# Two short expert calls of an attention and mixture-of-experts kernel: one of them is moved out of a branch, both now stand behind the fifth and the sixth pair of blocks

## The chip, the cores and the metric

The kernel runs on one core of one Trainium2 chip. The metric is the time of one execution in microseconds (us), as the device measures it. The program computes first an attention layer and then a routed mixture of experts, in one launch.

## The reference

The attention has 4 batches, 8 heads, 768 positions and 64 columns for each head; each position sees a window of its neighbours and 24 block summaries. Its output is cut into rows of 512 columns, 3072 rows in all, and each row goes to one of eight experts:

```
e = fresh_e if (s == 0 or local_gate[b, s] < 0.5) else prev_e
h = np.maximum(x[b, s] @ w1[e], 0.0)      # 512 -> 1024
out[b, s] = p[e] * (h @ w2[e])            # 1024 -> 512
```

So which rows belong to which expert is known only while the program runs.

## The kernel before

The rows of an expert are gathered into blocks of 128 rows. The experts' part of the program works on blocks, each of them a "slot" with an expert and a list of rows; a program part of the routing works out the slots while the attention and the first blocks run, and writes them into `words` in SBUF.

**Pairs.** `pair` runs two blocks of one expert at once: 96 matmuls of the first layer (lines 1131 to 1133; tiles `bs<-xT`), then 48 of the second layer for each block (lines 1104 to 1106; `ba<-hT`), with the transposes of the next pair's rows (L1087; `bt<-ident,xg`) between them. Each product is made of three matmuls, since weights and rows are split into a high and a low part. Eight pairs are written out in straight-line code, without a condition on TensorE: the static part. Behind them stands the dynamic part: at each step the program reads a word and takes either a pair or `single` (one block alone, `If two > 0` and its `Else`, L1457), until no slots are left. In the run that is shown the first step of the dynamic part takes the `single`, then come two pairs, a second `single` and a last pair.

**Weights.** While a pair runs, the weights of the next expert are split from the stage buffers `stg` into high and low parts, by ScalarE (L1062), VectorE (L1065) and GpSimd (L1070), and the stage is then filled again by SyncE's queue (L1058), each under a condition on the expert being a new one. In the run that is shown the stage is requested in the seventh and the eighth pair and in the dynamic part.

**The 32-row calls.** Up to two experts have a remainder of under 32 rows. Such a remainder doesn't get a block: `few` computes it with its own weights. `few_in` requests the weights (`few_w`, two tiles of 2 MB, four requests of 1 MB), `few_gather` fetches the rows (GpSimd, L1197), `few_tx` transposes them (L1204) and `few` makes both layers (L1219, L1223, L1230) under a condition (L1431). In the program a call has 32 matmuls for each layer, and the trace shows each as two. There is one pair of weight tiles, so the weights of the second call can be requested only when the first call has read them. In the run that is shown both calls are needed.

**Order around the change.** Before, the first call's weights and rows are requested behind the fifth pair, and the call stands behind the sixth. The second call's first weight tile is requested behind the first call, its second tile behind the seventh pair, and the call itself stands in the dynamic part, at the head of its first step: once in the branch of the pair and once in that of the `single`, since only one of them runs.

Of the kernel before, what the change touches and what calls it, by code (L numbers as in the profile page):

```python
# [16 lines left out]
ENG = mybir.EngineType  # L17
# [14 lines left out]
KT, FT = DM // P, DF // P  # L32
G9 = E + 1
SLOTS = 42
PAIRS = 8
FEW = 32
FEWS = 2
ALL = SLOTS + FEWS
CALLS = 12
EARLY = 6  # L40
FEW_TX = 5
FIRST = 10
OOB = 4096
WARM = 44
# [25 lines left out]
class Kernel:  # L70
# [1167 lines left out]
    def run(self):  # L1238
# [35 lines left out]
        def freed():  # L1274
            st["free"] += 1
            have_rows(0, st["rows"])
# [6 lines left out]
        def stage_e1():  # L1283
            for w in range(2):
                refill(w, st["e1"])
# [41 lines left out]
        def reg(i, engines, hi):  # L1327
            return nc.values_load(self.words[0:1, i:i + 1], engines=engines, min_val=0, max_val=hi)

        def refill(w, nxt):  # L1330
            for h in range(2):
                self.fetch(st["stage"][w][:, 2048 * h:2048 * h + 2048], w, 2048 * h, 2048 * h + 2048, nxt)

        def split(w, chunks):
            for q in chunks:
                eng = nc.vector if SPLIT_BY[w][q] == "V" else nc.gpsimd
                self.split(w, q * CH, q * CH + CH, st["stage"][w][:, q * CH:q * CH + CH], eng)

        def calls(n):

            r = {}

            def start(s):
                while "words" not in st:
                    self.small(1, True)
                if s not in r:
                    r[s] = reg(s, (ENG.SP, ENG.Activation, ENG.DVE, ENG.Pool), 1), reg(SLOTS + s, (ENG.SP,), E - 1)
                return r[s]

            def weights(w, s, chunks):  # L1350
                if s == EARLY - 2:
                    split(w, chunks)
                    if chunks[-1] == NCH - 1:
                        st["spent"].append(w)
                        refills()
                if not EARLY <= s < SLOTS:
                    return
                new, nxt = start(s)
                with tc.If(new > 0):  # L1359
                    split(w, chunks)  # L1360
                    if chunks[-1] == NCH - 1:
                        refill(w, nxt)

            def mid(half):
                if n < SLOTS:
                    while st["next"] <= n + half:
                        self.small(1, True)
                    if half and n >= 2 * PAIRS:
                        with tc.If(reg(n + 1, (ENG.PE, ENG.Activation, ENG.DVE), 1) > 0):
                            self.tx(n + half, half)  # L1370
                    else:
                        self.tx(n + half, half)
                    freed()

            return mid, lambda *chunks: weights(0, n, chunks), lambda *chunks: weights(1, n, chunks)
# [11 lines left out]
        with ExitStack() as ctx:  # L1387
            self.fw = ctx.enter_context(tc.tile_pool(name="f_wk", bufs=1))
            sp = ctx.enter_context(tc.tile_pool(name="stage", bufs=1))
            places = ctx.enter_context(ExitStack())  # L1390
            self.gw = places.enter_context(tc.tile_pool(name="g_wk", bufs=1, side="right"))
            st["spent"] = []
            st["stage"] = [sp.tile([P, KT * DF], F32, name=f"stg{w}") for w in range(2)]

            if "e1" in st:
                stage_e1()

            def refills():
                if "words" in st:
                    while st["spent"]:  # L1400
                        refill(st["spent"].pop(0), st["words"])

            def have_words():
                st["words"] = reg(SLOTS + EARLY - 2, (ENG.SP,), E - 1)
                refills()

            self.have_words = have_words
            rest = chain(first, *(self.pair(i, *calls(2 * i + 2)) for i in range(1, FEW_TX)))
            while self.steps:
                next(rest, None)  # L1410
                self.flow(C_T)
            for _ in rest:
                pass
            assert "words" in st and self.have_p == SLOTS
            places.close()
            fp = ctx.enter_context(tc.tile_pool(name="few", bufs=1, side="right"))
            self.few_w = [fp.tile([P, KT * DF], F32, name=f"few_w{w}") for w in range(2)]
            self.few_x = fp.tile([FEW, DM], F32, name="few_x")
            self.few_xT = fp.tile([P, KT, FEW], F32, name="few_xT")

            def few_reg(j, engines, hi=1):
                return nc.values_load(self.few_words[0:1, j:j + 1], engines=engines, min_val=0, max_val=hi)

            def few_in(j, chunks):
                used, e = few_reg(j, (ENG.SP,)), few_reg(FEWS + j, (ENG.SP,), E - 1)
                with tc.If(used > 0):
                    for q in chunks:
                        self.few_in(q, e)

            def few(j):  # L1430
                with tc.If(used[j] > 0):  # L1431
                    self.few(j)

            self.few_gather(0)
            few_in(0, range(4))
            for i in range(FEW_TX, PAIRS):
                for k, _ in enumerate(self.pair(i, *calls(2 * i + 2))):
                    if k == 2 * FT:
                        if i == FEW_TX:
                            self.few_tx()  # L1440
                            self.few_gather(1)
                        if i == PAIRS - 1:
                            self.few_tx()
                if i == FEW_TX:
                    used = [few_reg(j, (ENG.PE, ENG.Activation, ENG.DVE, ENG.Pool)) for j in range(FEWS)]
                    nb = reg(2 * SLOTS, mybir.ALL_ENGINES, SLOTS)
                    few(0)
                    few_in(1, range(2))
                if i == FEW_TX + 1:
                    few_in(1, range(2, 4))  # L1450
            with ExitStack() as c:  # L1451
                for i in range(2 * PAIRS, SLOTS, 2):
                    if i >= 2 * CALLS:
                        c.enter_context(tc.If(nb > i - EARLY))
                    two = reg(i + 1, mybir.ALL_ENGINES, 1)
                    kept = dict(st)
                    with tc.If(two > 0) as full:  # L1457
                        if i == 2 * PAIRS:
                            few(1)
                        for _ in self.pair(i // 2, *calls(i + 2)):  # L1460
                            pass
                    st.update(kept)
                    with full.Else():
                        if i == 2 * PAIRS:
                            few(1)
                        self.single(i, *calls(i + 2))


# [81 lines left out]
```

## Time and profile before

| | |
|---|---|
| time, median of 3 runs | 463.37 us (462.78 to 464.55) |
| the profiled execution's own time | 466.23 us |
| its span in the trace | 464.5 us |
| TensorE busy | 424.6 us, 91% of the span |
| ScalarE, VectorE, GpSimd busy | 202.4, 250.5 and 216.8 us |

The span is what the trace shows from the first instruction to the last; the execution's own time has 1.73 us more. The profiled execution is 2.86 us longer than the median of the three timed runs. A share of busy time is a mean over stages that differ; what a change in one stage is worth is read from that stage.

### The profile page before, as it was taken

Reading aid. Unit: us, or ns where it says so; the run is one execution under the profiler, and the core shown is the slowest. Engines: PE = TensorE matmul, PEld = TensorE weight load, DVE = VectorE, ACT = ScalarE, POOL = GpSimd, SP = SyncE. Lnnn points to the kernel's source line nnn. Section 1 sums busy time; section 2 is a strip of 40 time slices with the busy share of each in tenths; the row PEclk is TensorE's granted clock in tenths of the full one; section 3 lists DMA queues with packets and bytes.
Section 4 is the critical chain, followed back from the end, with each engine's and each line's share of the span. In section 5 each row is a group of like instructions: output and inputs, shape, how many; then the busy total and the mean of one; then the engine's idle time right before and its main releaser. Section 6 shows DMA issues by size and latency. Waiting matters only on the chain. (4 is left out here: it accounts for less than half of the span.)

```text
span 464.5 us, 12258 instructions
## 1 busy us (share of the span) xinstructions
PE 424.6 (91%) x4512; PEld 369.0 (79%) x4512; DVE 250.5 (54%) x610; ACT 202.4 (44%) x454; POOL 216.8 (47%) x305
## 2 busy tenths in 40 slices
PE   7799989889699999999999999999959999999980
PEld 6588868767489798898989898989847898977960
DVE  5776797888855798993222222155441722356410
ACT  4788787887635125421212121154431821358200
POOL 2687676687404423932030312149491652097620
PEclk9989999999889999999999999999997999999996
DMA  8999989989230660472920202508974472058930
GB/s 307 368 384 389 387 253 404 394 318 324 89 141 2 236 262 25 157 285 82 359 73 24 68 30 76 206 25 280 347 265 179 148 283 94 0 205 294 344 124 26
DMA packets 24009, 95.87 MB, mean 206 GB/s; under 512 B 2895, under 2 KB 3537, under 8 KB 19313
## 3 DMA queue, kind: packets, MB, share of 16 engines
q1 hardware_dynamic: 19328, 80.30, 46.4%
q0 software_dynamic: 4448, 14.29, 9.2%
q8 instruction: 43, 0.70, 0.6%
q14 instruction: 46, 0.37, 0.2%
q10 hardware_dynamic: 144, 0.20, 0.1%
HBM read 82.20 MB, written 12.71 MB: 204 GB/s over the span
## 5 line engine op out<-in xcount | busy, mean ns | idle before, releaser
L1131 PE MATMUL bs<-xT,h 128*128 128x256 f32 x352 | 101.2, 287 | 0.0
L1133 PE MATMUL bs<-xT,l 128*128 128x256 f32 x352 | 99.8, 284 | 0.7 <-DVE l L1065 0.5
L1132 PE MATMUL bs<-xT,h 128*128 128x256 f32 x352 | 99.7, 283 | 0.2 <-DVE xT L1082 0.2
L1076 POOL DMA_INDIRECT xg<-x_dram,gidx x30 | 35.1, 1170 | 102.2 <-POOLq L1359 43.2
L1137 ACT ACTIVATE hT<-bs 128x512 fp32r<-128x512 f32 x44 | 26.3, 597 | 110.1 <-PE bs L1133 107.6
L1104 PE MATMUL ba<-h,hT 128*128 128x512 f32 x176 | 71.5, 406 | 0.4
L1106 PE MATMUL ba<-h,hT 128*128 128x512 f32 x176 | 68.8, 391 | 0.0
L1105 PE MATMUL ba<-l,hT 128*128 128x512 f32 x176 | 68.7, 391 | 0.0
L1133 PEld LDWEIGHTS bs<-xT,l 128*128 128x128 f32 x352 | 67.4, 191 | 1.3 <-DVE l L1065 1.3
L1131 PEld LDWEIGHTS bs<-xT,h 128*128 128x128 f32 x352 | 67.4, 191 | 1.1 <-issue 0.6
L1132 PEld LDWEIGHTS bs<-xT,h 128*128 128x128 f32 x352 | 67.4, 192 | 0.9 <-DVE xT L1082 0.7
L1139 DVE SCALAR_TENSOR_TENSOR hT<-bs,hT 128x512 fp32r<-128x512 f32 x44 | 30.3, 690 | 68.9 <-ACT hT L1137 57.8
L1070 POOL TENSOR_TENSOR l<-stg,h 128x256 fp32r<-128x256 f32 x72 | 63.1, 907 | 7.6 <-ACT h L1062 6.9
L291 ACT ACTIVATE pr<-bs,nm 128x120 f32<-128x120 f32 x192 | 51.7, 370 | 12.0 <-DVE nm L287 11.5
L1062 ACT CAST h<-stg 128x1024 fp32r<-128x1024 f32 x48 | 48.8, 1051 | 9.2 <-PE ba L1106 8.1
L1117 POOL DMA_INDIRECT out_dram<-yo,sidx x24 | 27.0, 1124 | 46.1 <-DVE yo L1116 17.2
L1065 DVE TENSOR_TENSOR l<-stg,h 128x1024 fp32r<-128x1024 f32 x30 | 40.7, 1367 | 13.5 <-ACT h L1062 10.3
L1104 PEld LDWEIGHTS ba<-h,hT 128*128 128x128 f32 x176 | 33.1, 188 | 7.5 <-ACT h L1062 0.6
L1106 PEld LDWEIGHTS ba<-h,hT 128*128 128x128 f32 x176 | 33.0, 188 | 7.3
L1105 PEld LDWEIGHTS ba<-l,hT 128*128 128x128 f32 x176 | 33.2, 189 | 5.5
L252 POOL COPY vw<-vs 24x384 f32<-24x384 f32 x64 | 32.3, 546 | 7.7 <-ACT vs L247 6.2
L287 DVE TENSOR_REDUCE nm<-bs 128x6 f32<-128x720 f32 x32 | 28.8, 901 | 9.2 <-ACT vs L247 4.0
(278 smaller groups left out, 681.8 us busy)
## 6 DMA issues: line engine op xcount, KB each, us to landing
stg<-in_w SPq DMA_DIRECT2D x28, 1024.0 KB, 6.7
vw<-in_vW SPq DMA_DIRECT2D x16, 780.0 KB, 7.4
few_w<-in_w SPq DMA_DIRECT2D x8, 1024.0 KB, 8.9
kp<-in_kT SPq DMA_DIRECT2D x16, 384.0 KB, 6.5
q<-in_qT SPq DMA_DIRECT2D x16, 384.0 KB, 7.0
vt<-in_vT SPq DMA_DIRECT2D x16, 384.0 KB, 7.5
x_dram<-xs SPq DMA_DIRECT2D x8, 768.0 KB, 5.1
wst<-in_w SPq DMA_DIRECT2D x8, 512.0 KB, 6.9
```

The costliest lines, as they stand in the source:

```text
L252: nc.gpsimd.tensor_copy(out=vw[n % 3][WL:W, t:t + NW // 4, :, 0:D], in_=vs.to_broadcast([NB, NW // 4, 2, D]))
L291: nc.scalar.activation(out=pr[:, h, u, :], in_=sp[:, h, u, :], func=AF.Exp, bias=nm[:, h, u:u + 1], scale=1.0)
L1062: self.nc.scalar.copy(out=hi, in_=src)
L1065: eng.tensor_tensor(out=lo, in0=src, in1=hi.bitcast(F32), op=ALU.subtract)
L1070: eng.tensor_tensor(out=lo[:, p], in0=src[:, p], in1=hi[:, p].bitcast(F32), op=ALU.subtract)
L1076: self.nc.gpsimd.indirect_dma_start(out=t, out_offset=None, in_=rows, in_offset=bass.IndirectOffsetOnAxis(ap=self.gidx[:, i:i + 1], axis=0))
L1104: nc.tensor.matmul(out=ps, lhsT=ah, rhs=wh, start=first, stop=False)
L1105: nc.tensor.matmul(out=ps, lhsT=ah, rhs=wl, start=False, stop=False)
L1106: nc.tensor.matmul(out=ps, lhsT=al, rhs=wh, start=False, stop=last)
L1131: nc.tensor.matmul(out=ps[:, j], lhsT=wh, rhs=xh, start=(k == 0), stop=False)
L1132: nc.tensor.matmul(out=ps[:, j], lhsT=wh, rhs=xl, start=False, stop=False)
L1133: nc.tensor.matmul(out=ps[:, j], lhsT=wl, rhs=xh, start=False, stop=(k == KT - 1))
```

## The change

Both calls stand in the static part now. The first call's weights are requested behind the fourth pair, its rows are transposed within the fifth, and it runs behind the fifth; the second call's four weight requests stand together behind the first call, and it runs behind the sixth pair. The dynamic part has no call left. The registers that say whether a call is needed, and how many slots there are, are loaded ahead of the fifth pair instead of behind the sixth.

```
-FEW_TX = 5
+FEW_TX = 4
             self.few_gather(0)
             few_in(0, range(4))
+            used = [few_reg(j, (ENG.PE, ENG.Activation, ENG.DVE, ENG.Pool)) for j in range(FEWS)]
+            nb = reg(2 * SLOTS, mybir.ALL_ENGINES, SLOTS)
             for i in range(FEW_TX, PAIRS):
+                j = i - FEW_TX
                 for k, _ in enumerate(self.pair(i, *calls(2 * i + 2))):
-                    if k == 2 * FT:
-                        if i == FEW_TX:
-                            self.few_tx()
-                            self.few_gather(1)
-                        if i == PAIRS - 1:
-                            self.few_tx()
-                if i == FEW_TX:
-                    used = [few_reg(j, (ENG.PE, ENG.Activation, ENG.DVE, ENG.Pool)) for j in range(FEWS)]
-                    nb = reg(2 * SLOTS, mybir.ALL_ENGINES, SLOTS)
-                    few(0)
-                    few_in(1, range(2))
-                if i == FEW_TX + 1:
-                    few_in(1, range(2, 4))
+                    if k == 2 * FT and j < FEWS:
+                        self.few_tx()
+                        if j < FEWS - 1:
+                            self.few_gather(j + 1)
+                if j < FEWS:
+                    few(j)
+                    if j < FEWS - 1:
+                        few_in(j + 1, range(4))
...
                     with tc.If(two > 0) as full:
-                        if i == 2 * PAIRS:
-                            few(1)
                         for _ in self.pair(i // 2, *calls(i + 2)):
                             pass
                     st.update(kept)
                     with full.Else():
-                        if i == 2 * PAIRS:
-                            few(1)
                         self.single(i, *calls(i + 2))
```

On TensorE, at the end of the eighth pair, this stood before: the last matmul of the pair, the word that decides on pair or `single` (L1457), and in the branch of the pair the second call ahead of the pair's first matmul.

```order
L1106 MATMUL ba<-h_120,hT 128x512
L1359 UNCONDITIONAL_BRANCH
L1328 TENSOR_LOAD words
L1457 COMPARE_AND_BRANCH
L1431 COMPARE_AND_BRANCH
L1219 MATMUL bs<-few_w_4554,few_xT 32x128 x32
L1223 MATMUL bt<-ident,few_h 128x128 x2
L1230 MATMUL ba_5571<-few_w_4555,few_hT 32x128 x32
L1431 UNCONDITIONAL_BRANCH x2
L1131 MATMUL bs<-xT,h_119 128x256
```

Behind that pair's last matmul, and so at the far end of the jump, stood the `Else` before, again with the call ahead of the first matmul of the `single`; this is the copy that runs.

```order
L1106 MATMUL ba_5816<-h_120,hT 128x512
L1359 UNCONDITIONAL_BRANCH
L1457 UNCONDITIONAL_BRANCH
L1431 COMPARE_AND_BRANCH
L1219 MATMUL bs<-few_w_4554,few_xT 32x128 x32
L1223 MATMUL bt<-ident,few_h 128x128 x2
L1230 MATMUL ba<-few_w_4555,few_hT 32x128 x32
L1431 UNCONDITIONAL_BRANCH x2
L1104 MATMUL bs<-h_119,xT 128x512
```

In the changed program the second call stands on TensorE between the sixth pair's last matmul and the seventh pair's first, and nothing is jumped over to reach it.

```order
L1106 MATMUL ba<-h_120,hT 128x512
L1359 UNCONDITIONAL_BRANCH
L1431 COMPARE_AND_BRANCH
L1219 MATMUL bs<-few_w_4310,few_xT 32x128 x32
L1223 MATMUL bt<-ident,few_h 128x128 x2
L1230 MATMUL ba_5034<-few_w_4311,few_hT 32x128 x32
L1431 UNCONDITIONAL_BRANCH x2
L1131 MATMUL bs<-xT,h_119 128x256
```

What moved: the call, 66 matmuls in the program, left both branches and stands once in the straight line. The jump to the `Else` (its line is now L1455) is still there, over a branch that is shorter by the call.

On SyncE's queue the first tile of the second call's weights stood alone before, behind the condition on the call (L1426; `few_w_4554` is the first layer's tile, the next tile the second layer's).

```order
L1426 COMPARE_AND_BRANCH
L1058 ISA
L1058 DMA few_w_4554<-in_w 128x2048
L1058 ISA
L1058 DMA few_w_4554<-in_w 128x2048
L1426 UNCONDITIONAL_BRANCH x2
```

Now the four requests stand together.

```order
L1426 COMPARE_AND_BRANCH
L1058 ISA
L1058 DMA few_w_4310<-in_w 128x2048
L1058 ISA
L1058 DMA few_w_4310<-in_w 128x2048
L1058 ISA
L1058 DMA few_w_4311<-in_w 128x2048
L1058 ISA
L1058 DMA few_w_4311<-in_w 128x2048
L1426 UNCONDITIONAL_BRANCH x2
```

What moved: two requests of 1 MB that stood behind the seventh pair's stage requests stand now a pair and a half earlier, ahead of the sixth pair's stage conditions.

## Rows read from the trace of the kernel before

**Rows 1.** The page, first part: engine, busy us, share of the span, instructions.

```profile
PE   424.6 (91%) x4512; PEld 369.0 (79%) x4512; DVE 250.5 (54%) x610; ACT 202.4 (44%) x454; POOL 216.8 (47%) x305
```

**Rows 2.** The waits of TensorE: us in total, times, longest; the first row.

```profile
PE bs L1219 <- issue: 5.2, 1, 5.2
```

**Rows 3.** The timeline of TensorE at the second call: start, us, instructions, [idle before <-releaser].

```profile
340.74 0.39 PE L1106 MATMUL ba<-h,hT 128*128 128x512 f32 x1
341.44 1.47 PE L1219 MATMUL bs<-few_w,few_xT 128*32 128x128 f32 x43 [0.31 <-PE ba L1106]
348.15 1.50 PE L1219 MATMUL bs<-few_w,few_xT 128*32 128x128 f32 x21 [5.24 <-issue]
...
350.51 3.45 PE L1230 MATMUL ba<-few_w,few_hT 128*32 128x128 f32 x64
353.89 0.50 PE L1104 MATMUL bs<-h,xT 128*128 128x512 f32 x1
```

**Rows 4.** Windows of 1 us there: busy by engine, granted clock, DMA share, GB/s.

```profile
350.00:351.00 1.00, 0.99 (x14) 0.65 (x17) 0.58 (x2) 0.00 (x0) 0.80 (x1) 0.50 1.03 377
354.00:355.00 1.00, 1.00 (x5) 0.82 (x6) 0.35 (x1) 0.00 (x0) 0.00 (x0) 1.00 0.13 49
```

**Rows 5.** The DMA queues from 345 to 346 us: packets, MB, share; the instruction queue's row.

```profile
q8 instruction: 1, 0.02, 6.5%
```

**Rows 6.** The timeline of TensorE at the first call.

```profile
288.79 0.39 PE L1106 MATMUL ba<-h,hT 128*128 128x512 f32 x1
289.11 1.95 PE L1219 MATMUL bs<-few_w,few_xT 128*32 128x128 f32 x64
293.60 0.39 PE L1131 MATMUL bs<-xT,h 128*128 128x256 f32 x1
```

**Rows 7.** The timeline of TensorE: second single, and the pair behind it.

```profile
413.79 0.39 PE L1104 MATMUL bs<-h,xT 128*128 128x512 f32 x1
...
423.06 1.04 PE L1087 MATMUL bt<-ident,xg 128*128 128x128 f32 x8
...
426.70 0.28 PE L1131 MATMUL bs<-xT,h 128*128 128x256 f32 x1
...
439.34 0.40 PE L1104 MATMUL ba<-h,hT 128*128 128x512 f32 x1
```

**Rows 8.** The timeline of TensorE: the second layer begins behind the first single.

```profile
378.61 0.40 PE L1104 MATMUL ba<-h,hT 128*128 128x512 f32 x1
```

**Rows 9.** The timeline of VectorE: two splits ahead of the next pair, at either single.

```profile
365.90 2.36 DVE L1065 TENSOR_TENSOR l<-stg,h 128x1024 fp32r<-128x1024 f32 x2 [0.17 <-ACT h L1062]
...
425.81 3.17 DVE L1065 TENSOR_TENSOR l<-stg,h 128x1024 fp32r<-128x1024 f32 x2
```

**Rows 10.** The timeline of GpSimd: its split at either single.

```profile
362.80 2.91 POOL L1070 TENSOR_TENSOR l<-stg,h 128x256 fp32r<-128x256 f32 x4 [5.77 <-ACT h L1062]
...
423.92 2.84 POOL L1070 TENSOR_TENSOR l<-stg,h 128x256 fp32r<-128x256 f32 x4
```

**Rows 11.** The timeline of SyncE's queue: requests, their form and number.

```profile
220.48 71.17 SPq L1058 DMA_DIRECT2D few_w<-in_w  x6
314.42 10.30 SPq L1058 DMA_DIRECT2D stg<-in_w  x4
326.42 1.52 SPq L1058 DMA_DIRECT2D few_w<-in_w  x2
...
338.30 10.17 SPq L1058 DMA_DIRECT2D stg<-in_w  x4
...
411.18 9.63 SPq L1058 DMA_DIRECT2D stg<-in_w  x4
```

**Rows 12.** The tile few_w: its requests to landing.

```profile
DMA to landing us min/median/max: 5.2/8.9/12.7
```

**Rows 13.** Windows of the fifth and sixth pairs: as in rows 4.

```profile
265.00:270.00 5.00, 5.00 (x43) 4.96 (x43) 1.44 (x2) 0.60 (x1) 1.89 (x2) 1.00 0.20 69
270.00:284.00 14.00, 14.00 (x95) 12.49 (x94) 3.73 (x7) 2.97 (x5) 2.79 (x3) 1.00 0.09 23
```

## The prediction

> **What bounds the kernel now.** I read the page first: TensorE is busy for 424.6 of 464.5 us [rows 1], so the time can fall only where TensorE stands still, runs slowly, or does work that is left out. The change leaves no matmul out. So the waits of TensorE come next, and the longest single one lies in a 32-row call: 5.2 us in which nothing that the profile shows is waited for, "issue" [rows 2]. The timeline shows which call. The second call begins 0.70 us after the start of the eighth pair's last matmul, runs 43 matmuls, stands still from 342.91 to 348.15 us, and then runs the other 87 [rows 3]. The reader is to see two things there: the weights are not the reason, since the first 32 of the 64 matmuls of line 1219 read from both requests of that tile, and ran; and the matmuls behind the gap are slow. The windows say why they are slow: at 350 us the granted clock is 0.50 (the lower level, 1.2 GHz), and it is 1.00 again at 354 [rows 4]. TensorE had been idle for over 5 us before. The same call without any of this is the first one, behind the sixth pair: 64 matmuls in one piece of 1.95 us, no idle time [rows 6].
>
> What does the engine wait for? The queue that loads instructions moves one block at 345 to 346 us, in the gap [rows 5], while SyncE's stage requests from 338.30 us on fill the DMA queues [rows 11]; at 350 us their share is 1.03 [rows 4]. The call stands in the `Else`, at the far end of a jump. I read the gap as TensorE having used up the instructions that were there behind the jump and waiting for the next block, which came late behind 4 MB of weights.
>
> **The change part by part.**
>
> *The second call leaves the branch.* From the start of the pair's last matmul to the first matmul of the `single`: 353.89 - 340.74 = 13.15 us [rows 3]. The same stretch at the first call: 293.60 - 288.79 = 4.81 us [rows 6]. The call behind the sixth pair should cost what the first call costs, so 13.15 - 4.81 = 8.34 us go. They are made of the gap, 5.24; of the slow clock behind it (353.89 - 348.15 = 5.74 us for the rest of the call, where the first call has 4.49 - 1.47 = 3.02 left after as many matmuls), 2.72; and of 0.38 at the call's start (0.70 against 0.32).
>
> *The first call is moved by one pair.* Same work in the same straight line, no gain and no loss. The loads of the registers for both calls leave its front, where all that stands between the pair and the call is 0.32 us [rows 6]. They now stand ahead of the fifth pair. Bounds 0 and 0.3 us, either sign; I take 0.
>
> *The weights of the second call.* They can go out only when the first call has read the old ones. Two pairs lie between 293.60 us and 341 (their last matmul starts at 340.74) [rows 3, 6]: 23.7 us each, so the first call will run from 265.4 to 269.9 and the second from 293.6 on. Six `few_w` requests were issued early and two at 326.42 [rows 11]; a request lands 5.2 to 12.7 us after its issue [rows 12]. Even if all four go out at the end of the first call, 3 us apart in all (two took 1.52 to issue), and take the longest time, they land at 269.9 + 3 + 12.7 = 285.6 us, 8 us early. The DMA queues are nearly empty then: share 0.20 and 0.09 from 265 to 284 us [rows 13]. SyncE's queue stands at these requests until the first call has read its tiles; behind them wait the stage conditions of the sixth and the later pairs, whose first request came at 314.42 us [rows 11], so nobody is late by it. Cost 0; without this cover it would be what is missing of 23.7 us.
>
> *Two requests leave the eighth pair's time.* The 2 MB at 326.42 us shared the queues with the stage requests of 314.42 us on [rows 11]. No engine waits for these in the trace, so I count 0; the loss is excluded, since fewer bytes move there.
>
> *What the call was cover for.* Before, the `single` began 13 us after the pair; now it begins at once. While the call ran, GpSimd finished its splits of the second layer's weights and the stage filled up. What a `single` directly behind a pair costs stands in the trace: the second one, with the same stage requests just before (411.18 us, 2.6 us ahead of it; the new place has 338.30 against the pair's end at 341, 2.7 us) [rows 7, 11]. It and the next pair's first layer take 439.34 - 413.79 = 25.55 us [rows 7]; the first one takes 378.61 - 353.89 = 24.72 [rows 3, 8]. The difference, 0.83 us, has its place: VectorE's two splits ahead of the next pair take 3.17 instead of 2.36 us [rows 9], and GpSimd's split lies beside them there (423.92 to 426.76), but was over at 365.71, before VectorE's at 365.90 [rows 10]. I let the first `single` cost what the second does. Bounds: 0, if GpSimd is done in time, and 0.83, the value that I take.
>
> *Sum:* 8.34 - 0.83 = 7.5 us. On the profiled execution's own time, 466.23, that gives 458.7; that one lies 2.86 us over the median of the timed runs, so for the median I say 463.37 - 7.5 = **455.9 us**.
>
> **The rule that speaks against it.** The jump over the pair's branch stays, and [rows 3] show that a gap came behind it. The Trainium skill ("Runtime: NRT & Kernel Launch", section "Instruction fetch mechanics") says that instructions are loaded ahead in sequence only, and that a taken branch to a place that isn't loaded must load that place before the engine goes on. By that rule the wait would belong to the jump and not to the call, and would come back ahead of the `single`. The trace agrees in part: the gap lies behind a jump, but 43 matmuls behind it.
>
> **The rivals.**
>
> *The gap moves into the `single`* (on the other side). What decides is how many matmuls of the `single` run before the missing block is needed. The gap ended 348.15 - 341.44 = 6.71 us after the call's start [rows 3]. If 43 matmuls are there again, the `single` reaches its 45th only 423.06 - 413.79 = 9.27 us after its start (44 lie ahead of that row) [rows 7], since its matmuls are longer; so 2.6 us are to spare, and the second `single` shows no such gap. If the block is needed at once, 6.71 us and the slow clock, 2.72, come back: 463.37 - 7.51 + 9.43 = 465.3 us, slower. The sign turns where the wait is over 4.8 us, within the first 9 or so matmuls of the `single` (9.27 us for 44). Against it: the order of the code ahead of that place has the same length as before, one call in the straight line in place of one in the branch.
>
> *The call is starved wherever it stands:* short matmuls use up instructions fast (43 in 1.47 us), and the first call was only lucky with empty queues. Then gap and slow clock stay, 7.96 us, and the time is 463.37 - 7.51 + 7.96 = 463.8 us: the change does nothing. Against it stand the first call [rows 6] and the empty queues of the new place [rows 13]; the new 4 MB are through by 285.6 us.
>
> *The gap is shorter in the timed runs than in the profiled one*, which is 2.86 us longer as a whole. If all of these belong to the gap, 7.51 - 2.86 = 4.65 us are gained: 458.7 us. Nothing in the trace tells.
>
> **How the numbers follow.** Forecast 455.9: 0.72, of itself 454.5 to 457.5 (8.34 without the 0.83 gives 455.0, and the three runs before scatter by half a us downward). A shorter gap, or a part of it in the `single`, 457.5 to 460.5: 0.16. The starved call, 463.8: 0.06. The gap ahead of the `single`, 465.3: 0.04. Anything else: 0.02. The range 454.5 to 460.5 holds the first two. About 0.5%, 2.3 us, is what a measurement of this kernel can tell from no change; faster by more than that (under 461.05): 0.88, within it: 0.08, slower: 0.04.
>
> **What the next profile would show.** Both calls with 64 matmuls of line 1219 in one piece of 1.95 us and a granted clock of 1.00 behind them. No wait of over 1 us on "issue" on TensorE behind the eighth pair. The first matmul of the `single` within 0.7 us of the start of the pair's last. From there to the next pair's second layer 24.7 to 25.6 us. All four `few_w` requests of the second call landed before 286 us. The prediction is wrong if the clock drops behind the jump, if the second call waits for its weights, or if the first `single` waits for a split for over 1 us.

## The result and the profile after

| | before | after |
|---|---|---|
| timed runs, median | 463.96 us (462.78 to 464.69, 4 runs) | 458.12 us (456.88 to 458.8, 4 runs) |
| the profiled execution's own time | 466.23 us | 456.88 us |
| span in the trace | 464.5 us | 455.1 us |

The ratio is 0.9873, interval 0.9841 to 0.9906: 5.8 us faster, inside the range, 2.2 us above the forecast of 455.9. Of these, 0.6 us lie in the kernel before: the forecast started from its median of 463.37, and timed beside the kernel after it has 463.96.

The page's first part, for the kernel after; TensorE is 4.9 us less busy than in [rows 1] with the same 4512 matmuls.

```profile
PE 419.7 (92%) x4512; PEld 365.4 (80%) x4512; DVE 250.5 (55%) x610; ACT 202.6 (45%) x454; POOL 216.4 (48%) x305
```

The timeline of TensorE at the second call, now behind the sixth pair, and at the start of the first `single` (start, us, instructions), to be read against [rows 3] and [rows 6].

```profile
292.31 0.39 PE L1106 MATMUL ba<-h,hT 128*128 128x512 f32 x1
292.63 1.96 PE L1219 MATMUL bs<-few_w,few_xT 128*32 128x128 f32 x64
294.51 0.80 PE L1223 MATMUL bt<-ident,few_h 128*128 128x128 f32 x2
295.24 1.96 PE L1230 MATMUL ba<-few_w,few_hT 128*32 128x128 f32 x64
297.12 0.39 PE L1131 MATMUL bs<-xT,h 128*128 128x256 f32 x1
...
343.71 0.39 PE L1106 MATMUL ba<-h,hT 128*128 128x512 f32 x1
343.93 0.39 PE L1104 MATMUL bs<-h,xT 128*128 128x512 f32 x1
```

Windows there, in the columns of [rows 4]: behind the call, and at the start of the `single`.

```profile
297.00:298.00 1.00, 1.00 (x15) 0.88 (x8) 0.35 (x1) 0.00 (x0) 0.11 (x1) 1.00 0.07 16
...
344.00:347.00 3.00, 3.00 (x15) 2.49 (x14) 2.40 (x2) 1.20 (x2) 3.00 (x4) 1.00 1.01 407
```

From the pair's last matmul to the next work the second call takes 297.12 - 292.31 = 4.81 us, to the hundredth what the first call took before; it took 13.15. The `single` follows the eighth pair after 0.22 us at a clock of 1.00, although the stage requests fill the DMA queues (share 1.01).

The jump to the `Else` is still there, but it takes less time. The part of TensorE that reads the program (its sequencer, `PEldq`) has a record of the jump: its duration three times in ns, then its start in us. Before:

```profile
L1457 PEldq COMPARE_BRANCH  x1: 3648/3648/3648, 337.3 to 337.3; - x1
```

After, with the row of the queue that loads instructions from 341.2 to 343 us:

```profile
L1455 PEldq COMPARE_BRANCH  x1: 340/340/340, 340.3 to 340.3; - x1
```

```profile
q8 instruction: 1, 0.02, 3.3%
```

Before, the jump was reached 3.4 us ahead of the pair's last matmul and lasted 3.65 us, to 341.0; a block moved at 338.3. After, it lasts 0.34 us and is over at 340.6, while that queue moves nothing from 335.2 to 341.2 us. So the block that it leads to was there already, and the block at 341.4 is the one behind. The branch that is jumped over has become shorter by the call, 260 instructions as the trace shows them (130 matmuls, each with its weight load). That this is why the target was there is a reading; no run changed the length of the jump alone.

The waits of TensorE: the row of [rows 2] has no successor; the only wait behind the attention that comes near 1 us is this one.

```profile
PE bs L1133 <- DVE l L1065: 1.3, 2, 0.8
```

It is made of two waits: 0.51 us at 358.93, behind the first `single`, where before had none, and 0.80 behind the second, where before had 0.51. The first of them is the small price that was foreseen. VectorE's two splits ahead of the next pair, and GpSimd's beside them, which answer to [rows 9] and [rows 10]:

```profile
356.10 2.78 DVE L1065 TENSOR_TENSOR l<-stg,h 128x1024 fp32r<-128x1024 f32 x2
```

```profile
353.80 2.85 POOL L1070 TENSOR_TENSOR l<-stg,h 128x256 fp32r<-128x256 f32 x4
```

They overlap for half a microsecond; from the start of the `single` to the next pair's second layer 369.21 - 343.93 = 25.28 us pass, against 24.72 before: 0.56 us given back.

```profile
369.21 0.40 PE L1104 MATMUL ba<-h,hT 128*128 128x512 f32 x1
```

The weights: SyncE's queue issued the last of the eight `few_w` requests at 268.7 us, and the slowest request took 11.6 us, so all was there by 280.3, 12 us ahead of the call. The second tile's two requests, at 326.42 us in [rows 11], stand behind the fifth pair now instead of the seventh, so two pairs earlier and not one and a half. SyncE's timeline, and the tile's requests to landing:

```profile
218.73 50.35 SPq L1058 DMA_DIRECT2D few_w<-in_w  x8
```

```profile
DMA to landing us min/median/max: 4.9/9.1/11.6
```

### The profile page after: what moved, and what is told of

It is laid out like the page before. It is cut to its first block, busy times and chain, and to the rows that moved or that the text cites. A ratio compares the mean times of both kernels' runs of the same rounds, so it can differ in the third digit from the quotient of the medians.

```text
span 455.1 us, 12196 instructions
## 1 busy us (share of the span) xinstructions
PE 419.7 (92%) x4512; PEld 365.4 (80%) x4512; DVE 250.5 (55%) x610; ACT 202.6 (45%) x454; POOL 216.4 (48%) x305
## 5 line engine op out<-in xcount | busy, mean ns | idle before, releaser
L1076 POOL DMA_INDIRECT xg<-x_dram,gidx x30 | 33.7, 1124 | 100.7 <-PE bt L1087 43.2
L1070 POOL TENSOR_TENSOR l<-stg,h 128x256 fp32r<-128x256 f32 x72 | 66.2, 952 | 2.1 <-ACT h L1062 1.2
L291 ACT ACTIVATE pr<-bs,nm 128x120 f32<-128x120 f32 x192 | 51.9, 371 | 11.6 <-DVE nm L287 8.3
L1117 POOL DMA_INDIRECT out_dram<-yo,sidx x24 | 25.4, 1060 | 47.0 <-DVE yo L1116 16.9
```

Source lines behind the costliest of these rows:

```text
L291: nc.scalar.activation(out=pr[:, h, u, :], in_=sp[:, h, u, :], func=AF.Exp, bias=nm[:, h, u:u + 1], scale=1.0)
L1070: eng.tensor_tensor(out=lo[:, p], in0=src[:, p], in1=hi[:, p].bitcast(F32), op=ALU.subtract)
L1076: self.nc.gpsimd.indirect_dma_start(out=t, out_offset=None, in_=rows, in_offset=bass.IndirectOffsetOnAxis(ap=self.gidx[:, i:i + 1], axis=0))
```

## The experiments

Two theories stood against each other. **A:** behind the jump there are instructions for one block and no more; short matmuls use them up before the next block is there, and long ones don't. The place relative to the jump, the block's border and the length of the matmuls decide. **B:** a 32-row call is starved by its own short matmuls whenever the DMA queues are full; the change gains because the queues are empty at the new place. A third reading gives the gain to the weights' requests that went together.

### A second look at the kernel before

No edit.

> The kernel before, unchanged, for a second trace of it. If the gap in the second call is a fixed thing, it has again 43 matmuls ahead of it and is 5 to 6 us long, and the call's stretch is about 13 us. If the timed runs gain less than the traces show because the gap varies, it is shorter here, 3 to 4 us, with a span near 462.

463.97 us (10 runs), ratio 0.9992, interval 0.9964 to 1.0019. The timeline of TensorE at the second call:

```profile
339.03 0.39 PE L1106 MATMUL ba<-h,hT 128*128 128x512 f32 x1
339.60 1.47 PE L1219 MATMUL bs<-few_w,few_xT 128*32 128x128 f32 x43 [0.19 <-PE ba L1106]
345.22 1.50 PE L1219 MATMUL bs<-few_w,few_xT 128*32 128x128 f32 x21 [4.15 <-issue]
...
351.15 0.72 PE L1104 MATMUL bs<-h,xT 128*128 128x512 f32 x1
```

The gap stands behind the 43rd matmul again, but is 4.15 us, not 5.24. The place is fixed and the length varies. The pair's last matmul began at 339.03, so the stretch up to the `single` is 351.15 - 339.03 = 12.12 us here, 13.15 in the execution of [rows 3]. This execution's own time, 463.8, lies at the median.

### After, a second time

No edit.

> The changed kernel, unchanged, timed more often beside the kernel before, and with a second trace. The first traces of the two put 7.9 us on the stretch from the fifth pair to the last matmul, the first timed runs only 5.8. My reading after the second trace of the kernel before: the gap varies from run to run (5.2 and 4.2 us in two traces), so the timed runs should gain 6 to 7 us, ratio 0.985 to 0.988, and this trace should show no gap again. If the trace was a lucky one, a gap of some us stands in this one behind the eighth pair or in a call.

458.36 us (6 runs), ratio 0.9865, interval 0.9829 to 0.99. No gap; from the `single` to the next pair's second layer 25.31 us. The stretch from the fifth pair's first matmul to the end of the last matmul of all measures 201.76 and 201.71 us in the two traces of after, 209.63 and 208.94 in those of before: 7.2 to 7.9 us less. The rest of the difference between the two first spans (9.4 us) lies ahead of the fifth pair, and differs as much between two traces of one kernel: that pair begins at 241.67 and 239.97 us before, at 239.92 and 241.53 after.

### Does the second call starve under full queues?

The kernel after, with both calls a pair later. The second now falls into the stage requests of the seventh pair.

```
-FEW_TX = 4
+FEW_TX = 5
```

> The changed kernel with FEW_TX = 5 again: both calls still in the static part, but behind the sixth and the seventh pair, so that the first call isn't moved at all and the second runs while the stage requests of the seventh pair fill the DMA queues (from 314 us on). If the gain comes from the way out of the branch alone: same time as the changed kernel, 457 to 459, both calls without a gap. If short matmuls starve when the queues are full: a gap of 1 us or more in the second call, 460 to 463.

457.92 us (6 runs), ratio 0.9853, interval 0.9819 to 0.9887, as after. The timeline of TensorE and the window of the call:

```profile
319.49 1.96 PE L1219 MATMUL bs<-few_w,few_xT 128*32 128x128 f32 x64
...
322.12 1.96 PE L1230 MATMUL ba<-few_w,few_hT 128*32 128x128 f32 x64
```

```profile
319.00:324.00 5.00, 4.86 (x133) 3.79 (x131) 2.99 (x4) 1.87 (x4) 4.96 (x6) 1.00 0.97 369
```

With the DMA queues at 0.97 the call runs in one piece. Full queues alone don't starve it, in straight-line code. Theory B falls for that case, and which pair the first call follows has no part in the gain.

### Are the weights' requests part of the gain?

The kernel after, with the second tile requested in the middle of the sixth pair.

```
+                        else:
+                            few_in(j, range(2, 4))
                 if j < FEWS:
                     few(j)
                     if j < FEWS - 1:
-                        few_in(j + 1, range(4))
+                        few_in(j + 1, range(2))
```

> The changed kernel, but the second call's weights are not requested together: its second tile only in the middle of the sixth pair, some 12 us ahead of the call. If it doesn't matter how they are requested as long as they land in time: same time as the changed kernel, 457 to 459, and no wait of TensorE for a tile. If requesting them early is part of the gain: a wait for the second layer's weights in the second call, 1 to 4 us, 460 to 463.

457.4 us (4 runs), ratio 0.9846, interval 0.9803 to 0.9889. No wait for a tile. Requesting them together neither gains nor costs.

### The call out of the branch, but directly ahead of the jump

The kernel before, with the second call in the static part behind the eighth pair.

```
+                if i == PAIRS - 1:
+                    few(1)
...
                     with tc.If(two > 0) as full:
-                        if i == 2 * PAIRS:
-                            few(1)
...
                     with full.Else():
-                        if i == 2 * PAIRS:
-                            few(1)
```

> The kernel before with one edit: the second call stands in the static part behind the eighth pair, so at the same time as before and under the same stage requests (4 MB from 338 us on), but with no jump ahead of it. My theory (the gap is the wait for an instruction block behind a jump): 64 matmuls of line 1219 in one piece of about 2 us, no gap, clock 1.00; the call costs 4.8 us instead of 13.15, and the single behind it finds its splits done, so about 8 us less than before: 455 to 457. Rival (the short matmuls starve wherever the DMA queues are full): a gap of about 5 us stays in the call and the time is that of before, 463 to 465.

> Edit: none against call_behind_8th (the second call in the static part behind the eighth pair); a second trace and a second timing. There the trace saved 4 to 5 us against the kernel before and the timed runs showed nothing (463.2 against 464.2). If the trace was one of a short gap, this one shows a gap ahead of the single that is longer than 3.4 us, or stands behind its first matmuls, or pulls the clock to 0.50, and the timed runs say 461 to 464 again. If the trace is typical, the gap is 3 to 4 us again at a clock of 1.00 and the timed runs should come down to 459 to 461.

463.21 us (10 runs), ratio 0.9992, interval 0.9967 to 1.0016; the second time 461.94 us (8 runs), ratio 0.9949, interval 0.9926 to 0.9972. The timeline of TensorE in the second trace:

```profile
339.69 1.95 PE L1219 MATMUL bs<-few_w,few_xT 128*32 128x128 f32 x64
...
347.95 0.47 PE L1104 MATMUL bs<-h,xT 128*128 128x512 f32 x1 [3.66 <-issue]
...
349.12 0.63 PE L1105 MATMUL bs<-l,xT 128*128 128x512 f32 x1
```

The call itself is clean, and the gap stands behind it, ahead of the `single`: it belongs to the jump, whose own record lasts 3.44 and 3.67 us here. The expectation of no gap and 455 to 457 us failed. Moving the call out of the branch gains 1.0 us, which isn't clear of the noise, or 3.0; the rest of the 5.8 comes with moving it away from the jump. The first trace shows 3.42 us at the same place:

```profile
349.03 0.47 PE L1104 MATMUL bs<-h,xT 128*128 128x512 f32 x1 [3.42 <-issue]
```

What follows the gap differs. In the first trace the granted clock stayed at 1.00 behind it; in the second it fell to 0.50 within a microsecond (matmuls of 0.63 instead of 0.39 us). Windows of the 4 us behind the gap, of the second trace, then of the first:

```profile
348.00:352.00 4.00, 4.00 (x11) 3.19 (x12) 0.00 (x0) 0.00 (x0) 0.00 (x0) 0.60 0.94 337
```

```profile
349.00:353.00 4.00, 3.97 (x18) 3.31 (x19) 0.00 (x0) 0.60 (x1) 0.29 (x1) 1.00 0.95 317
```

The stretch from the fifth pair on is 204.85 and 206.26 us, 4.1 to 4.8 us under before in the first trace and 2.7 to 3.4 in the second; the timed runs gave 1.0 and 3.0 us. The second pair of numbers agrees. Why the first timing shows next to nothing stays open.

### The call in the branch, behind long matmuls

The kernel before, with the call behind the `single` (and behind the pair in the other branch).

```
                     with full.Else():
+                        self.single(i, *calls(i + 2))
                         if i == 2 * PAIRS:
                             few(1)
-                        self.single(i, *calls(i + 2))
```

> Edit: in the kernel before, the second call stays in both branches of the dynamic part's first step, but stands behind the step's work instead of ahead of it. If the gap belongs to short matmuls directly behind a jump, the 9.3 us that the first 44 matmuls of the single take now cover the block's load: no wait on issue of over 1 us behind the eighth pair, 64 matmuls of line 1219 in one piece, granted clock 1.00, and the time 457 to 460 us, less what the call costs ahead of the next pair's splits (up to 1.5 us, either sign). If a call in a branch is starved by its own short matmuls wherever the queues are full, a gap of 3 to 5 us comes inside the call, now behind the single, and the time stays at 463 to 464.

460.38 us (6 runs), ratio 0.9907, interval 0.9882 to 0.9933. The `single` starts 0.23 us behind the pair, and the call has all 64 matmuls in one piece, with the DMA queues at 0.84 around it. TensorE's timeline, ScalarE's, and a window:

```profile
353.13 1.95 PE L1219 MATMUL bs<-few_w,few_xT 128*32 128x128 f32 x64
357.10 0.64 PE L1223 MATMUL bt<-ident,few_h 128*128 128x128 f32 x2 [2.01 <-DVE l L1065]
358.46 3.64 PE L1230 MATMUL ba<-few_w,few_hT 128*32 128x128 f32 x64 [0.72 <-DVE few_hT L1224]
362.03 0.58 PE L1131 MATMUL bs<-xT,h 128*128 128x256 f32 x1
```

```profile
351.09 5.78 ACT L1062 CAST h<-stg 128x1024 fp32r<-128x1024 f32 x6
356.77 0.45 ACT L1220 ACTIVATE few_h<-bs 128x128 f32<-128x128 f32 x2
```

```profile
350.00:355.00 5.00, 5.00 (x81) 4.05 (x78) 4.05 (x5) 4.90 (x7) 4.82 (x6) 1.00 0.84 277
```

Theory A foresaw that there is no gap, in a branch and with busy queues, although the jump goes as far as before and lasts 3.31 us. Of a new cost in the call its expectation had 1.5 us at most, and a clock of 1.00; both failed. The wait of 2.01 us is put down to VectorE, but the transposes of line 1223 need `few_h`, which ScalarE makes at 356.77, behind six weight casts that stand ahead of it in its queue. With that and the clock, which fell behind this wait (0.65 from 357 to 358 us, 0.50 in the next), the call takes 362.03 - 353.13 = 8.90 us instead of 4.49. So the gain is 4.6 us where the change gains 5.8.

### Does the block's border set the place?

The kernel before, with 48 matmuls of zeros at the end of the pair's branch in the dynamic part's first step. That branch isn't taken, so they never run; they only move the jump's target.

```
                         for _ in self.pair(i // 2, *calls(i + 2)):
                             pass
+                        if i == 2 * PAIRS:
+                            self.pad(48)
```

> The kernel before with 48 matmuls of zeros added at the end of the pair's branch of the first dynamic step, which isn't taken in this run: nothing more is executed, only the jump goes 96 instructions further. My theory: blocks of instructions have fixed borders in the program. The place behind the jump lies now just behind a border, so the whole block of 256 instructions is there, and the call, 260 instructions by the trace's count, runs to about its last matmuls of the second layer before it must wait; the gap moves from behind the 43rd matmul of line 1219 into line 1230 or behind it, and shrinks from 5.2 us to 2 to 3 us: 1 to 4 us faster than before. Rival (starved by full queues, borders play no part): the gap stays behind about 43 matmuls and 5 us long, same time as before.

459.81 us (8 runs), ratio 0.9901, interval 0.9872 to 0.993: matmuls that don't run make the kernel 4.4 us faster. The timeline of TensorE at the call (lines are five higher, 1235 is 1230):

```profile
340.30 1.95 PE L1224 MATMUL bs<-few_w,few_xT 128*32 128x128 f32 x64
342.18 0.79 PE L1228 MATMUL bt<-ident,few_h 128*128 128x128 f32 x2
342.96 1.74 PE L1235 MATMUL ba<-few_w,few_hT 128*32 128x128 f32 x56
345.47 0.42 PE L1235 MATMUL ba<-few_w,few_hT 128*32 128x128 f32 x8 [0.77 <-issue]
```

The gap moved from behind 43 matmuls to behind 64 + 2 + 56 = 122, and shrank to 0.77 us (2 to 3 were expected), since these took time to run. The place agrees with fixed borders: 79 matmuls later, each with its weight load, are 158 instructions; the pad adds 96 ahead; together 254, the length of one block if the borders are regular. The page counts the blocks that the queue for instructions moves; its row in after gives 16 KB each:

```profile
q8 instruction: 42, 0.69, 0.6%
```

With the wait nearly gone, VectorE's two splits ran beside GpSimd's and took 4.85 us where [rows 9] show 2.36, and the next pair's first layer waited 1.78 and 0.52 us for them.

```profile
357.96 4.85 DVE L1065 TENSOR_TENSOR l<-stg,h 128x1024 fp32r<-128x1024 f32 x2 [0.17 <-ACT h L1062]
```

### Can the border undo the change?

The kernel after, with 168 such matmuls, 336 instructions. By the count of the experiment before, these are one block and 82 more, where 86 instructions (43 matmuls with their weight loads) lay between target and border: a handful is left.

```
+                        if i == 2 * PAIRS:
+                            self.pad(168)
```

> The changed kernel with 168 matmuls of zeros added at the end of the pair's branch of the first dynamic step, which isn't taken: nothing more is executed, the jump to the first single goes 336 instructions further, so that it lands some 10 instructions ahead of a border of two blocks, and the block that it lands in isn't the next one any more. My theory: the first single stops after 4 or 5 matmuls for 5 to 7 us, its clock falls, and most of the gain is lost: 464 to 468. This is the rival of the prediction in which the gap moves into the single, made on purpose. Rival theory (the gap belongs to the call with its short matmuls, not to the jump): the single runs as in the changed kernel, 457 to 459.

463.48 us (10 runs), ratio to before 0.9992, interval 0.9966 to 1.0017: the whole gain is gone. TensorE at the start of the `single`, and two windows:

```profile
345.87 0.47 PE L1104 MATMUL bs<-h,xT 128*128 128x512 f32 x1 [0.20 <-PE ba L1106]
...
346.63 0.40 PE L1104 MATMUL bs<-h,xT 128*128 128x512 f32 x1
351.97 0.80 PE L1105 MATMUL bs<-l,xT 128*128 128x512 f32 x1 [4.93 <-POOL l L1070]
```

```profile
345.00:351.00 6.00, 1.83 (x7) 0.88 (x6) 2.48 (x2) 1.50 (x2) 5.85 (x7) 0.98 0.93 326
351.00:357.00 6.00, 5.03 (x12) 3.97 (x13) 0.00 (x0) 0.60 (x1) 2.46 (x4) 0.50 1.00 386
```

Four matmuls, then 4.93 us of nothing and a clock of 0.50. The page puts the wait down to GpSimd; that is the last event before it, not what the matmul needs, since the only thing changed is where the code lies. Two things follow from that edit at once: the border lies close behind the target, and the longer jump itself lasts 3.85 us again, not 0.34. This is the first rival of the prediction, the gap ahead of or early in the `single`, brought about by an edit.

### How much of the gap is DMA traffic?

The kernel before, without the four stage requests of the eighth pair. This leaves out the loading of 4 MB of weights.

```
-                    if chunks[-1] == NCH - 1:
+                    if chunks[-1] == NCH - 1 and s != 2 * PAIRS:
                         refill(w, nxt)
```

> The kernel before without the four stage requests of the eighth pair (4 MB); the next step then splits the weights that the stage held already, so this kernel leaves out loading them. The jump, the call and the borders of the blocks are as before. If the block of instructions is late because it queues behind the stage's 4 MB: the gap behind the 43rd matmul shrinks from 4 or 5 us to under 1.5, the clock stays at 1.00, and the time falls by 5 to 8 us, to 456 to 459. If the load of the block takes that long by itself: the gap stays at 4 to 5 us and the time at 463 to 464.

461.25 us (8 runs), ratio 0.9915, interval 0.9887 to 0.9943.

```profile
342.32 1.50 PE L1219 MATMUL bs<-few_w,few_xT 128*32 128x128 f32 x43
346.01 0.85 PE L1219 MATMUL bs<-few_w,few_xT 128*32 128x128 f32 x21 [2.20 <-issue]
```

```profile
342.00:346.00 4.00, 1.82 (x45) 1.23 (x43) 2.49 (x2) 1.46 (x3) 3.99 (x5) 1.00 0.42 139
```

Same place, 2.20 us instead of 4.15 and 5.24, and the clock keeps 1.00; the time falls by 3.1 us. Both lie between the two expectations. I read some 2 to 3 us of the gap as the block's queueing behind the stage's weights, and the rest as the block's own way; this is one trace. In it the queue for instructions moves two blocks here, at 339.6 and 343.8 us, 4.2 us apart; in the two traces of before they are 6.2 and 7.5 apart.

## Why the prediction was right, and where it was 2.2 us off

**The cause** was read rightly: TensorE had used up what was there behind the jump and waited for the next block of instructions. The pads show it by themselves, since they move code and nothing else: the gap follows the border, 43 matmuls behind the target, or 122, or 4. The theory that a short call starves wherever the queues are full fell with the calls behind the sixth and seventh pair, and with the call behind the `single`.

**The second call leaves the branch** (8.34 us): at the new place it costs exactly the 4.81 us that the prediction took over from the first call. The other side of the subtraction was mis-sized. 13.15 us came from one execution, whose gap of 5.24 us was long; the second trace has 12.12. With it the term is 12.12 - 4.81 = 7.31.

**What the call was cover for** (0.83 us): 0.56 measured against the `single` of [rows 3, 8]. The place was right, VectorE's splits beside GpSimd's. The second trace of before has 376.09 - 351.15 = 24.94 us for this stretch, against which 0.34 are lost.

**The sum** with the second trace of before is 7.31 - 0.34 = 7.0 us, where the forecast had 7.5; the four timings of the change and of its two harmless variants gave 5.8, 6.0, 6.4 and 6.9. So the step that failed is the one that took the profiled execution's gap off the median, though that execution was 2.86 us longer than the median. The rival that gave all of this to the gap said 458.7, near what came, and in part by luck. It named the reason rightly and overdid it: the gap differs by 1.1 us between the two traces of before, and of the 2.4 us between their execution times 1.7 lie ahead of the fifth pair; its gain of 4.65 us is under all four timings, and 0.6 us of its nearness come from the kernel before, which was timed slower beside the kernel after. The mean of the four timings is 6.3; the 0.7 us from there to 7.0 are within what they tell.

**The weights, the moved first call, the requests that left the eighth pair** were taken at 0; the two variants with the calls a pair later and with the weights apart time the same as after, so nothing contradicts it.

**The rule that spoke against the change.** In before the jump waited for its target's block, 3.65 us in the first trace and 3.59 in the second, but TensorE had matmuls of the pair to run until 341.1; the wait that cost time came at the next border, as the prediction held against the rule. With the call directly ahead of the jump the block came at 346.5 and 345.3 us in the two traces, behind the call's last matmul, and the wait stood at the jump itself, although the branch there is as short as in after. The Trainium skill ("Runtime: NRT & Kernel Launch", section "Instruction fetch mechanics") says of a taken branch whose target isn't among the loaded instructions that the target's block must be fetched before the engine goes on. The traces agree: where a block is moved during the jump, the jump lasts 3.31 to 3.85 us, and in after and its two harmless variants, where none is, 0.34 to 0.36. Whether it costs anything depends on how long the matmuls queued ahead of the jump run.

The rival in which the gap comes back early in the `single` was given 0.04. Against it stood the argument that the code ahead of that place keeps its length, so that the target stays where it was in its block. What the prediction didn't see is that the jump becomes shorter by the call and finds its target loaded: the following block moved at 341.4 us, ahead of most of the stage's traffic (DMA share 0.06 from 341 to 342 us) and before the `single` began at 343.93, so more than the reckoned 2.6 us were to spare. This was luck, but the gain doesn't need it: with the call behind the `single` the jump lasts 3.31 us, and still no gap comes. The 168 matmuls show how much hung on it.

**Open:** the first timing with the call directly behind the eighth pair, which shows 3 us less than its trace; where a block spends the 2 us that are left without the stage's traffic; and what the shorter jump is worth by itself.

## What to carry to other kernels

Behind a jump, ask what TensorE runs while the next block of instructions is on its way: long matmuls cover it, a handful of short ones don't, and this holds ahead of the jump as well as behind it. Put short work in straight-line code, away from jumps; and where a kernel's time moves by 1% for an edit that seems to do nothing, look whether code behind a jump was shifted against a block's border. Take a gap from two executions before it enters a sum with decimals.

## What the runs showed of the hardware

- A stretch of code that never runs changed the time by 4.4 us one way (48 matmuls) and by 5.4 us the other (168 matmuls, 463.48 against 458.12, timed on two occasions).
- The jump over the first dynamic pair lasted 3.65 us on TensorE's sequencer before and 0.34 us after; before, TensorE had queued matmuls enough to cover nearly all of it.
- The wait for a block depends on the DMA traffic: 2.20 us without the stage's 4 MB, 4.15 and 5.24 with it.
- The length of one wait doesn't settle the clock: 3.42 us of idle at a jump left it at 1.00 and 3.66 at the same jump brought 0.50, but in the call behind the `single` it fell behind a wait of 2.01 us.
- VectorE's two splits took 2.36 us alone, 2.78 and 3.17 with GpSimd's split partly beside them, 4.85 with nearly the whole of it beside them.
